# A tuned attention and mixture-of-experts kernel: the weights' maxima over the partitions go from TensorE and VectorE to a GpSimd library call

## The chip, the cores and the metric

The kernel runs on one core of one Trainium2 chip. A core has TensorE (PE in the profile, with its weight loads as PEld), VectorE (DVE), ScalarE (ACT), GpSimd (POOL) and SyncE (SP), which issues the DMAs. Each engine takes its instructions in the order of its own program and waits at semaphores for the others. The metric is the device time of one execution in microseconds, the median over runs.

## The reference

Three layers follow one another, all in float32:

```python
# 1. clustered attention: q, k, v (2, 8, 768, 64); a score counts only where the
#    nearest of 16 centroids of the query and of the key is the same one
# 2. h = x @ w_in; g = h * clip(h + 3, 0, 6) / 6; x = g @ w_out      (1536 tokens, 512 -> 2048 -> 512)
# 3. eight experts, all of them for every token:
    logits = x @ w_gate
    P = np.exp(logits - logits.max())
    for _ in range(8):
        P /= P.sum(1, keepdims=True) + 1e-09
        P /= P.sum(0, keepdims=True) + 1e-09
        P *= N / E
    for e in range(E):
        h = np.maximum(x @ w1[e], 0.0)      # 512 -> 1024
        out += P[:, e:e + 1] * (h @ w2[e])  # 1024 -> 512
```

## The kernel before

TensorE multiplies float16. A float32 matrix is therefore scaled by a power of two and split into a high and a low float16 part, and three products of parts stand for one float32 product. The power of two comes from the largest absolute value of the whole matrix. So before a weight can be split, one number has to be found over all 128 partitions and be known on each of them.

How that number is found: the pieces of a weight matrix are reduced along each partition by VectorE as they come (`amax`, L235 for a second weight w2 and L1308 for a first weight w1), eight values a partition in the tile `mx`. `top_steps` (L92) makes the rest in five steps: (a) VectorE reduces the eight to one in a column of the tile `pad` (L99); (b) TensorE transposes `pad` into spare columns of a PSUM bank (L75); (c) VectorE reduces the 128 columns to the maximum (L80); (e) TensorE multiplies that by the identity, which puts it on every partition (L85, two records each); and the last step hands it to `scale_of` (L121 to L130), which makes the scale `ws_s`. Beside the weights, `top_steps` serves other tensors (`x2`, the logits `lg`, the gate).

The third layer runs as 64 units, `unit(u)`, eight for each expert e: four quarters of the hidden features by two halves of the tokens. A unit has seven products (L1488 to L1491, six matmuls of 384 columns each) that build two PSUM accumulators X and Y, a Strassen-like scheme of seven products instead of eight. ScalarE copies an accumulator when a partial sum is needed later (`snap`, L1496), VectorE adds it (`u`, L1503), ScalarE and VectorE make the hidden parts `hh` and `hl` (L1507, L1508). The bank of a unit's Y becomes the X of the next unit. Behind each product stands a slot, `fill(0)` to `fill(6)`, with one or two groups of three matmuls of 512 columns of the unit before (L1437 to L1439, the second weight's product), and with whatever the plan puts there.

`plan_expert(e)` (L1401) writes the plan for expert e, while expert e-1 is computed: `at2(u, slot, f)` puts a step behind a slot's matmul groups, `at2_first` ahead of them, and `at_hops` puts the five steps of `top_steps` half a slot apart. With u = 8 (e - 1), the second weight w2 (names `w{n}_1`, printed `w_1_...` in the order below) has its last partial maximum in unit u+1, slot 4, and its five steps in slots 5 and 6 of that unit and slot 0 of the next; it is then split from unit u+2 on (L244 on ScalarE, L247 on VectorE). The first weight w1 (`w{n}_0`) has its last partial maximum in unit u+4, slot 6, and its steps in slots 0 to 2 of unit u+5. Its four quarters are then combined by GpSimd (`c0`, `c1`, tiles `cmb`, L1325 to L1331), scaled by ScalarE (`hi`, L1340, into `wop`) and completed by VectorE (`lo`, L1344): quarter 0 from slot 2 of unit u+5, its `hi` of the combined rows in slot 6.

GpSimd also makes four differences of the input for the second half of the tokens, for each token half (`diff`, L1066, tiles `xt`, by number T1 to T4); those of the second half lie in the first units of expert 0, beside the plan of expert 1. ScalarE (`hi`, L1079) and VectorE (`lo`, L1086) split them.

Of the kernel before, what the change touches and what calls it, by code (L numbers as in the profile page):

```python
# [8 lines left out]
F32 = mybir.dt.float32  # L9
# [4 lines left out]
ALU = mybir.AluOpType  # L14
AX = mybir.AxisListType
PSUM = bass.MemoryType.PSUM

P = 128
NJ = 6
# [11 lines left out]
def attention_moe_kernel(  # L31
# [16 lines left out]
    nc = tc.nc  # L48
# [43 lines left out]
    def top_steps(cols, col, name, room, then):  # L92


        d = {}

        def a():
            x = cols()
            nc.vector.tensor_reduce(pad[:, col:col + 1], x, axis=AX.X if len(x.shape) == 2 else AX.XY, op=ALU.max)  # L99

        def b():
            d["rows"], start = room(P)
            red_rows(d["rows"], start)

        def c():
            d["r"] = red_max(d.pop("rows"), name)

        def e():
            d["m"], start = room(1)
            to_all(d.pop("r"), d["m"], start, col)  # L110

        return [a, b, c, e, lambda: then(d.pop("m"))]

    def scale_of(m, n, target, name, keep, cap=None, bufs=1):

# [82 lines left out]
    def weight_tasks(n, m, pool, raw=None):  # L198

        src = layers[n][m]  # L200
        wide = src.dtype != F32
        rows, cols = src.shape
        nr = rows // P
        NP = 8
        d = {}
        nm = f"w{n}_{m}"

        def view(t, i):

            return t.rearrange("p a f -> p (a f)")[:, 512 * i:512 * (i + 1)]  # L210

        def start():
            d["raw"] = raw
            if raw is None:
                d["raw"] = mp.tile([P, nr, cols], F32, tag="raw", name=f"{nm}_raw", bufs=1)
            d["mx"] = small.tile([P, NP], F32, tag="w_mx", name=f"{nm}_mx")
            if not wide:
                nc.sync.dma_start(d["raw"], src.rearrange("(c p) f -> p c f", p=P))

        def load(i):  # L220
            r, o = divmod(512 * i, cols)
            d["c", i] = wide_tile(
                wdec2, src[P * r:P * r + P, o:o + 512].bitcast(U32), f"{nm}_c{i}", [512], bufs=WB)

        def dec0(i):
            d["t", i] = decode0(wdec2, d["c", i], f"{nm}_t{i}", bufs=3)

        def dec1(i):
            decode1(d["t", i])

        def dec2(i):
            decode2(d.pop(("c", i)), d.pop(("t", i)), view(d["raw"], i))

        def amax(i):
            nc.vector.tensor_reduce(  # L235
                d["mx"][:, i:i + 1], view(d["raw"], i), axis=AX.X, op=ALU.max, apply_absolute_value=True)

        def scale1(m1):
            d["s"], wsc[n, m] = scale_of(m1, 1, 2 + m, f"ws{m}", small, bufs=4)
            wsp[n, m] = pool.tile(  # L240
                [P, 2, nr, cols], F16, tag="ws", name=f"{nm}_s", bufs=1 if pool is wpool else 2)

        def hi(i):
            nc.scalar.activation(view(wsp[n, m][:, 0], i), view(d["raw"], i), AF.Copy, scale=d["s"][:, 0:1])  # L244

        def lo(i):
            nc.vector.scalar_tensor_tensor(  # L247
                out=view(wsp[n, m][:, 1], i), in0=view(d["raw"], i), scalar=d["s"][:, 0:1],
                in1=view(wsp[n, m][:, 0], i), op0=ALU.mult, op1=ALU.subtract)

        def piece(i):
            if not wide:
                return idle, idle, idle, idle, lambda: amax(i), idle
            return (lambda: load(i), lambda: dec0(i), lambda: dec1(i), lambda: dec2(i), lambda: amax(i), idle)

        def lo_pool(i):

            v = view(d["raw"], i)
            nc.scalar.activation(v, v, AF.Copy, scale=d["s"][:, 0:1])
            nc.gpsimd.tensor_tensor(out=view(wsp[n, m][:, 1], i), in0=v, in1=view(wsp[n, m][:, 0], i), op=ALU.subtract)  # L260

        parts = []
        for i in range(NP):
            parts += [(0.05, lambda i=i: hi(i)), (0.2, lambda i=i: lo_pool(i)) if (n, m) == (1, 0) else (0.7, lambda i=i: lo(i))]
        scale = top_steps(lambda: d["mx"], 1, nm, spare if n > 2 else room1, scale1)
        return start, [("m", piece(i)) for i in range(NP)], scale, parts

    def pipeline(pieces, depth):
# [655 lines left out]
    for g in range(-LEAD, NU + LAG + 16):  # L924
        i, u = divmod(g, NJ)
# [371 lines left out]
    def expert_w1(e):  # L1297

        n = 2 + e
        d = {}  # L1300

        def load():
            d["raw"] = mp.tile([P, KD, 1024], F32, tag="raw", name=f"w{n}_0_raw", bufs=1)
            d["mx"] = small.tile([P, 8], F32, tag="w_mx", name=f"w{n}_0_mx")
            nc.sync.dma_start(d["raw"], w1[e].rearrange("(c p) f -> p c f", p=P))

        def amax(i):
            nc.vector.tensor_reduce(  # L1308
                d["mx"][:, i:i + 1], d["raw"][:, i // 2, 512 * (i % 2):512 * (i % 2) + 512],
                axis=AX.X, op=ALU.max, apply_absolute_value=True)  # L1310

        def scale1(m1):
            d["s"], wsc[n, 0] = scale_of(m1, 1, 2, "ws0", small, bufs=4)

        def pair(i):
            x = {}

            def a(f, c):
                o = P * (i + 4 * f)
                return d["raw"][:, 2 * c:2 * c + 2, o:o + P]  # L1320

            def c0():
                s = x["s"] = epool.tile([P, 4, 2, P], F32, tag="cmb", name=f"cmb{e}_{i}", bufs=2)
                x["w"] = wop[e, i] = epool.tile([P, 2, 7, 2, P], F16, tag="wop", name=f"wop{e}_{i}", bufs=5)
                nc.gpsimd.tensor_tensor(out=s[:, 0], in0=a(1, 0), in1=a(1, 1), op=ALU.add)  # L1325
                nc.gpsimd.tensor_tensor(out=s[:, 2], in0=a(0, 0), in1=a(1, 0), op=ALU.subtract)

            def c1():
                s = x["s"]
                nc.gpsimd.tensor_tensor(out=s[:, 1], in0=s[:, 0], in1=a(0, 0), op=ALU.subtract)  # L1330
                nc.gpsimd.tensor_tensor(out=s[:, 3], in0=a(0, 1), in1=s[:, 1], op=ALU.subtract)  # L1331

            def parts():
                yield slice(A11, A12 + 1), d["raw"][:, :, P * i:P * i + P].rearrange("p (a c) f -> p a c f", a=2)
                yield A22, a(1, 1)
                yield slice(S1, S4 + 1), x["s"]

            def hi(k):
                o, v = list(parts())[k]
                nc.scalar.activation(x["w"][:, 0, o], v, AF.Copy, scale=d["s"][:, 0:1])  # L1340

            def lo(k):
                o, v = list(parts())[k]
                nc.vector.scalar_tensor_tensor(  # L1344
                    out=x["w"][:, 1, o], in0=v, scalar=d["s"][:, 0:1], in1=x["w"][:, 0, o],
                    op0=ALU.mult, op1=ALU.subtract)

            return [
                (0.1, c0), (0.1, c1), (0.1, lambda: hi(0)), (0.7, lambda: (lo(0), hi(1))),
                (0.4, lambda: (lo(1), hi(2))), (1.2, lambda: lo(2))]  # L1350

        return (
            load, [(0.65, lambda i=i: amax(i)) for i in range(8)],
            top_steps(lambda: d["mx"], 1, f"w{n}_0", spare if e else room1, scale1),
            [pair(i) for i in range(4)])


# [32 lines left out]
    def at2(u, slot, f):  # L1390
        plan2.setdefault((u, slot), []).append(f)
# [4 lines left out]
    def at_hops(u, slot, steps):  # L1396

        for n, f in enumerate(steps):
            v, k = divmod(slot + (n + 1) // 2, 7)
            (at2 if n % 2 == 0 else at2_first)(u + v, k, f)  # L1400

    def plan_expert(e):

        u = 8 * (e - 1)
        start, pcs, sc, parts = prep_matrix(2 + e, 1)
        at2(u - 1, 6, start)
        for k, (_, p) in enumerate(pcs):
            at2(u + (k + 4) // 7, (k + 4) % 7, p[4])
        at_hops(u + 1, 5, sc)
        for k in range(8):  # L1410
            at2(u + 2 + k // 7, k % 7, parts[2 * k][1])
            at2(u + 2 + (k + 1) // 7, (k + 1) % 7, parts[2 * k + 1][1])
        load, mx, sc, prs = expert_w1(e)
        at2(u + 3, 2, load)
        for k, f in enumerate(mx):
            at2(u + 4, max(0, k - 1), f[1])
        at_hops(u + 5, 0, sc)
        for i, (v, k) in enumerate(((5, 2), (6, 0), (6, 4), (7, 1))):
            for f in prs[i]:
                at2(u + v, k, f[1])  # L1420
                v, k = (v, k + 1) if k < 6 else (v + 1, 0)
# [131 lines left out]
    for u in range(NU2):  # L1553
        e = u // 8
# [53 lines left out]
```

## Time and profile before

| what | value |
|---|---|
| median of 3 runs | 1584.22 us (1580.78 to 1585.2) |
| profiled execution, its own time | 1583.48 us |
| its span, first to last instruction | 1581.7 us |
| TensorE busy | 1441.0 us, 91% of the span |
| VectorE busy | 975.2 us, 62% |
| ScalarE busy | 653.4 us, 41% |
| GpSimd busy | 345.6 us, 22% |
| DMA queue of the data | 86.15 MB, 19.9% of 16 engines' span |

Busy time adds up an engine's instructions. Matmuls are pipelined and their modelled records overlap: a matmul of 512 columns has a record of 0.38 us, and the next one starts 0.22 us later. What TensorE loses is therefore read from the distance between the starts of neighbouring matmuls and not from busy time. The expert stage lies from about 600 us to the end.

### The profile page before, as it was taken

To read this page: it belongs to the slowest core of one execution; us is meant where nothing else is said; L and a number is where in the kernel's file an instruction comes from. 1 tells how busy PE (TensorE), PEld (TensorE's weight loads), DVE (VectorE), ACT (ScalarE), POOL (GpSimd) and SP (SyncE) were. 2 spreads that over 40 slices of the span, in tenths; PEclk is the share of its full clock that TensorE was granted. 3 is DMA by queue.
4 is the path that set the end of the run, shared out by engine and by line. 5 is a ranking of instruction groups with operands and counts; after the bars stand their busy time and mean duration, and the time that the engine had idled before them with its cause. 6 is when DMAs were issued, how large, how long until landed. Compare 5 with 4: busy or idle time off the path is not lost.

```text
span 1581.7 us, 22923 instructions
## 1 busy us (share of the span) xinstructions
PE 1441.0 (91%) x9331; PEld 771.8 (49%) x9331; DVE 975.2 (62%) x1769; ACT 653.4 (41%) x1088; POOL 345.6 (22%) x313
## 2 busy tenths in 40 slices
PE   3778877897999798989999999999999999999999
PEld 1456555543444344445555555555555555555554
DVE  7888878886765667565456455455555554655332
ACT  2667756455443344334334323323323323324221
POOL 1568867443110321100010020020011011011000
PEclk9989978798999999999999999999999999999999
DMA  9387453231311010101101101101001011010011
GB/s 221 78 153 168 84 106 68 56 130 43 130 46 59 30 54 1 54 1 53 54 1 54 54 0 54 46 9 54 25 30 53 5 50 53 1 54 1 1 40 41
DMA packets 106633, 87.60 MB, mean 55 GB/s; under 512 B 78368, under 2 KB 88608, under 8 KB 106528
## 3 DMA queue, kind: packets, MB, share of 16 engines
q1 hardware_dynamic: 106528, 86.15, 19.9%
q8 instruction: 73, 1.20, 0.3%
q14 instruction: 32, 0.26, 0.1%
HBM read 64.01 MB, written 3.15 MB: 42 GB/s over the span
## 4 chain that ended last, share of the span: by engine, by line
PE 70%; DVE 20%; ACT 4%; issue 3%; DMA 1%; SPq 0%; DVEq 0%; ACTq 0%
PE o L1437 10%; PE o L1439 10%; PE o L1438 10%; PE X L1488 5%; PE X L1491 5%; PE X L1490 5%; PE Y L1491 4%; PE Y L1488 4%; PE Y L1490 4%; DVE pmt L650 3%; PE l L1220 3%; PE pmt L647 2%; PE l L888 2%; PE l L889 2%; PE l L890 1%
## 5 line engine op out<-in xcount | busy, mean ns | idle before, releaser
L1439 PE MATMUL o<-w_s,hl 128*128 128x512 f16 x768 | 291.9, 380 | 0.0
L1438 PE MATMUL o<-w_s,hh 128*128 128x512 f16 x768 | 291.8, 380 | 0.0
L1437 PE MATMUL o<-w_s,hh 128*128 128x512 f16 x768 | 291.7, 380 | 0.0
L1507 ACT ACTIVATE hh<-u 128x384 f16<-128x384 f32 x192 | 100.3, 523 | 373.3 <-DVE u L1503 373.3
L1325 POOL TENSOR_TENSOR cmb<-w_raw 128x256 f32<-128x256 f32 x32 | 24.1, 753 | 822.9 <-DMA w_raw<-in_moe_w_dram 379.5
L718 POOL TENSOR_TENSOR El<-E,Eh 128x768 f16<-128x768 f32 x92 | 160.8, 1758 | 115.5 <-ACT Eh L716 50.3
L1508 DVE SCALAR_TENSOR_TENSOR hl<-u,hh 128x384 f16<-128x384 f32 x192 | 112.3, 585 | 113.1 <-ACT hh L1507 113.1
L1503 DVE TENSOR_TENSOR u<-X,snap 128x384 f32<-128x384 f32 x64 | 35.7, 557 | 194.7 <-PE X L1491 194.7
L1490 PEld LDWEIGHTS <-wop 128*128 128x128 f16 x896 | 87.8, 98 | 88.1 <-issue 8.2
L1488 PEld LDWEIGHTS <-wop 128*128 128x128 f16 x896 | 87.8, 98 | 81.8 <-issue 0.7
L1503 DVE TENSOR_TENSOR u<-Y,snap 128x384 f32<-128x384 f32 x128 | 70.7, 552 | 82.0 <-PE Y L1491 82.0
L1439 PEld LDWEIGHTS <-hl 128*128 128x128 f16 x768 | 75.2, 98 | 91.1 <-issue 0.8
L1220 PE MATMUL l<-hh,w_s 128*128 128x512 f16 x384 | 118.6, 380 | 0.0
L704 ACT ACTIVATE E<-pS,esc 128x768 f32<-128x768 f32 x96 | 86.2, 898 | 77.1 <-PE pS L700 73.9
L1491 PEld LDWEIGHTS <-wop 128*128 128x128 f16 x896 | 87.7, 98 | 58.2 <-issue 0.3
L1496 ACT COPY snap<-X 128x384 f32<-128x384 f32 x128 | 61.2, 478 | 124.2 <-PE X L1491 122.8
L1437 PEld LDWEIGHTS <-hh 128*128 128x128 f16 x768 | 78.0, 102 | 64.8 <-issue 0.3
L1438 PEld LDWEIGHTS <-hh 128*128 128x128 f16 x768 | 75.2, 98 | 65.1 <-issue 0.4
L650 DVE TENSOR_REDUCE pmt<-pmt 128x1 f32<-128x768 f32 x84 | 80.7, 961 | 30.2 <-PE pmt L647 29.2
L647 PE MATMUL pmt<-kA,qA 80*128 80x384 f16 x184 | 53.4, 377 | 48.5 <-DVE pmt L650 20.4
L1220 PEld LDWEIGHTS <-w_s 128*128 128x128 f16 x576 | 56.6, 99 | 68.1 <-issue 1.1
L1488 PE MATMUL X<-xop,wop 128*128 128x384 f16 x256 | 83.4, 326 | 2.3 <-DVE u L1503 0.9
(280 smaller groups left out, 2997.5 us busy)
## 6 DMA issues: line engine op xcount, KB each, us to landing
w_raw<-in_moe_w_dram SPq DMA_DIRECT2D x16, 2048.0 KB, 8.8
w_c<-in_moe_w_out_dram SPq DMA_DIRECT2D x16, 512.0 KB, 3.6
w00x<-in_moe_w_in_dram SPq DMA_DIRECT2D x8, 512.0 KB, 5.6
w00f<-in_moe_w_in_dram SPq DMA_DIRECT2D x8, 512.0 KB, 3.8
w_c<-in_moe_w_in_dram SPq DMA_DIRECT2D x8, 512.0 KB, 3.9
qraw<-in_q_dram SPq DMA_DIRECT2D x8, 384.0 KB, 3.6
kraw<-in_k_dram SPq DMA_DIRECT2D x8, 384.0 KB, 4.2
vraw<-in_v_dram SPq DMA_DIRECT2D x2, 1536.0 KB, 9.9
```

What stands on the lines that cost most here:

```text
L650: nc.vector.tensor_reduce(nmx[i][:, j:j + 1], ps[:, :, 0:N2], axis=AX.XY, op=ALU.max, negate=True)
L718: eng.tensor_tensor(out=El, in0=E, in1=Eh, op=ALU.subtract)
L1220: nc.tensor.matmul(po[i], lhsT=a, rhs=r, start=(f == 0 and z == 0), stop=(f == NFC - 1 and z == 2))
L1437: nc.tensor.matmul(pe2[t], lhsT=a, rhs=wh, start=first, stop=False)
L1438: nc.tensor.matmul(pe2[t], lhsT=a, rhs=wl, start=False, stop=False)
L1439: nc.tensor.matmul(pe2[t], lhsT=b, rhs=wh, start=False, stop=last)
L1488: nc.tensor.matmul(o[:, 0:XT], lhsT=wh, rhs=xh, start=(first and c == 0), stop=False, skip_group_check=True)
L1490: nc.tensor.matmul(o[:, 0:XT], lhsT=wh, rhs=xl, start=False, stop=False, skip_group_check=True)
L1491: nc.tensor.matmul(o[:, 0:XT], lhsT=wl, rhs=xh, start=False, stop=(c == 1), skip_group_check=True)
L1503: nc.vector.tensor_tensor(h, src, r[k], op=ALU.add)
L1507: nc.scalar.activation(hh, src, AF.Relu)
L1508: nc.vector.scalar_tensor_tensor(out=hl, in0=src, scalar=0.0, in1=hh, op0=ALU.max, op1=ALU.subtract)
```

## The change

For the two weights of experts 1 to 7, fourteen maxima, the five steps become two. In the first, `partition_all_reduce` on GpSimd takes the tile `mx` (128 partitions by 8) and writes to every partition, column by column, the maximum over the partitions. In the second, one slot later, VectorE reduces these eight to one and calls `scale_of`. The weights of expert 0, of the second layer and all other users keep `top_steps`.

```diff
@@ -110,6 +111,21 @@
             to_all(d.pop("r"), d["m"], start, col)
 
         return [a, b, c, e, lambda: then(d.pop("m"))]
+
+    def top_library(cols, name, then):
+
+        d = {}
+
+        def a():
+            d["m8"] = small.tile([P, 8], F32, tag="w_m8", name=f"{name}_m8")
+            nc.gpsimd.partition_all_reduce(d["m8"], cols(), channels=P, reduce_op=RED.max)
+
+        def b():
+            m1 = small.tile([P, 1], F32, tag="w_m1", name=f"{name}_m1")
+            nc.vector.tensor_reduce(m1, d.pop("m8"), axis=AX.X, op=ALU.max)
+            then(m1)
+
+        return [a, b]
...
-        scale = top_steps(lambda: d["mx"], 1, nm, spare if n > 2 else room1, scale1)
+        scale = top_library(lambda: d["mx"], nm, scale1) if n > 2 else top_steps(
+            lambda: d["mx"], 1, nm, room1, scale1)
         return start, [("m", piece(i)) for i in range(NP)], scale, parts
...
-            top_steps(lambda: d["mx"], 1, f"w{n}_0", spare if e else room1, scale1),
+            top_library(lambda: d["mx"], f"w{n}_0", scale1) if e else top_steps(
+                lambda: d["mx"], 1, f"w{n}_0", room1, scale1),
             [pair(i) for i in range(4)])
...
-        at_hops(u + 1, 5, sc)
+        at2(u + 1, 5, sc[0])
+        at2(u + 1, 6, sc[1])
...
-        at_hops(u + 5, 0, sc)
+        at2(u + 5, 0, sc[0])
+        at2(u + 5, 1, sc[1])
```

The call belongs to another GpSimd library than `tensor_tensor`, so the program that is built holds loads of libraries, which the code does not show. They stand as `ISA` without names ahead of the instruction that needs them. In GpSimd's order around expert 1's two maxima stood before the last two of the differences (`xt`) and the combinations of the first quarter:

```order
L1066 TENSOR_TENSOR xt_1_7151<-acc,xt_1_7094 128x768
L1066 TENSOR_TENSOR xt_1_7193<-acc 128x768
L1325 TENSOR_TENSOR cmb_0_7772<-w_0_raw 128x256
L1326 TENSOR_TENSOR cmb_0_7772<-w_0_raw 128x256
L1330 TENSOR_TENSOR cmb_0_7772<-cmb_0_7772,w_0_raw 128x256
```

and now, in the changed kernel's line numbers:

```order
L1083 TENSOR_TENSOR xt_1_7151<-acc,xt_1_7094 128x768
L121 ISA
L121 ISA w_1_m_7173<-w_1_mx 128x8
L1083 ISA
L1083 TENSOR_TENSOR xt_1_7200<-acc 128x768
L121 ISA
L121 ISA w_0_m_7699<-w_0_mx 128x8
L1342 ISA
L1342 TENSOR_TENSOR cmb_0_7770<-w_0_raw 128x256
L1343 TENSOR_TENSOR cmb_0_7770<-w_0_raw 128x256
L1347 TENSOR_TENSOR cmb_0_7770<-cmb_0_7770,w_0_raw 128x256
```

Expert 1 has four loads. The last difference (T3) now stands behind a call and two loads, and the combinations of quarter 0 behind the second call and a load. For experts 2 to 7 there are two loads each, one ahead of w2's call, behind the fourth quarter's combinations of the expert before, and one ahead of the combinations of quarter 0: sixteen loads in all.

On TensorE, at the end of a unit in which w2's maximum is made (expert 2's), stood the transpose between a product and the group behind it, and the broadcast behind the next product:

```order
L1491 MATMUL X_8241<-xop_6633,wop_1_7883 128x384
L75 MATMUL Y_8260<-ident,pad 128x128
L1437 LDWEIGHTS hh_2_8228
L1437 MATMUL o_0_2_8326<-w_1_s,hh_2_8228 128x512
...
L1491 MATMUL X_8366<-xop_6633,wop_2_7956 128x384
L85 MATMUL X_8366<-ident,w_1_r 128x1
L1437 LDWEIGHTS hh_3_8322
```

and now there:

```order
L1511 MATMUL X_8371<-xop_6633,wop_2_7954 128x384
L1457 LDWEIGHTS hh_2_8355
L1457 MATMUL o_0_2_8324<-w_1_s,hh_2_8355 128x512
L1458 LDWEIGHTS hh_2_8355
L1458 MATMUL o_0_2_8324<-w_1_s,hh_2_8355 128x512
```

Nothing but the 28 instructions of the steps (b) and (e) left TensorE's program. On VectorE stood at the same place:

```order
L1508 SCALAR_TENSOR_TENSOR hl_1_8340<-u_1_8337,hh_1_8339 128x384
L99 TENSOR_REDUCE pad<-w_1_mx 128x1
L1508 SCALAR_TENSOR_TENSOR hl_2_8357<-X_8241,hh_2_8356 128x384
L80 TENSOR_REDUCE w_1_r<-Y_8260 128x1
L121 TENSOR_SCALAR ws_e<-X_8366 128x1
L122 TENSOR_SCALAR ws_e<-ws_e 128x1
```

and now:

```order
L1528 SCALAR_TENSOR_TENSOR hl_1_8338<-u_1_8335,hh_1_8337 128x384
L1528 SCALAR_TENSOR_TENSOR hl_2_8356<-X_8239,hh_2_8355 128x384
L125 TENSOR_REDUCE w_1_m_8362<-w_1_m_8347 128x1
L137 TENSOR_SCALAR ws_e<-w_1_m_8362 128x1
L138 TENSOR_SCALAR ws_e<-ws_e 128x1
```

The reduction that waits for the call stands where the reduction of the transposed column stood, and the four steps of the scale follow it at once.

## Rows read from the trace of the kernel before

**Rows 1.** Page: chain of work that ended last, shares of the span by engine.
```profile
PE 70%; DVE 20%; ACT 4%; issue 3%; DMA 1%; SPq 0%; DVEq 0%; ACTq 0%
```

**Rows 2.** Stretch: length; PE, PEld, DVE, ACT, POOL busy; clock, DMA share, GB/s.
```profile
820.00:940.00 120.00, 117.70 (x628) 61.05 (x627) 64.76 (x117) 44.44 (x82) 11.68 (x16) 1.00 0.10 36
```

**Rows 3.** One line's instructions: duration ns min/median/max, first and last start (us).
```profile
L75 PE MATMUL Y<-ident,pad x15: 327/330/332, 622.1 to 1411.3; 128*128 128x128 f32 x15
```

**Rows 4.** Timeline of TensorE, w2's steps: start us, us, instruction [idle <- releaser].
```profile
878.01 0.33 PE L1491 MATMUL X<-xop,wop 128*128 128x384 f16 x1
878.59 0.33 PE L75 MATMUL Y<-ident,pad 128*128 128x128 f32 x1 [0.26 <-DVE pad L99]
...
881.40 0.38 PE L85 MATMUL X<-ident,w_r 128*128 128x1 f32 x2 [0.57 <-ACT snap L1496]
881.65 0.38 PE L1437 MATMUL o<-w_s,hh 128*128 128x512 f16 x1
```

**Rows 5.** Timeline of TensorE, the same place two units on, without such steps.
```profile
894.46 0.33 PE L1491 MATMUL X<-xop,wop 128*128 128x384 f16 x1
...
896.24 0.38 PE L1437 MATMUL o<-w_s,hh 128*128 128x512 f16 x1
```

**Rows 6.** Timeline of TensorE, w1's steps.
```profile
927.54 0.33 PE L1491 MATMUL Y<-xT,wop 128*128 128x384 f16 x1
928.58 0.33 PE L75 MATMUL Y<-ident,pad 128*128 128x128 f32 x1 [0.72 <-DVE u L1503]
...
931.81 0.38 PE L85 MATMUL X<-ident,w_r 128*128 128x1 f32 x2 [0.62 <-ACT snap L1496]
932.05 0.38 PE L1437 MATMUL o<-w_s,hh 128*128 128x512 f16 x1
```

**Rows 7.** Timeline of TensorE, the same slots one unit on, without such steps.
```profile
944.21 0.33 PE L1491 MATMUL Y<-xT,wop 128*128 128x384 f16 x1
...
945.67 0.33 PE L1488 MATMUL X<-xT,wop 128*128 128x384 f16 x1
...
946.64 0.38 PE L1437 MATMUL o<-w_s,hh 128*128 128x512 f16 x1
```

**Rows 8.** Timeline of VectorE: w2's last partial maximum and its scale; w1's last partial maximum.
```profile
876.17 0.68 DVE L235 TENSOR_REDUCE w_mx<-w_raw 128x1 f32<-128x512 f32 x1
881.82 0.16 DVE L121 TENSOR_SCALAR ws_e<-X 128x1 int32<-128x1 int32 x1 [2.18 <-PE X L85]
...
926.39 0.68 DVE L1308 TENSOR_REDUCE w_mx<-w_raw 128x1 f32<-128x512 f32 x1
```

**Rows 9.** Timeline of ScalarE: quarter 0's combined rows, and the copy behind them.
```profile
941.07 1.14 ACT L1340 ACTIVATE wop<-cmb,ws_s 128x1024 f16<-128x1024 f32 x1
942.30 0.48 ACT L1496 COPY snap<-X 128x384 f32<-128x384 f32 x1
```

**Rows 10.** One tile's instructions (cmb): duration ns min/median/max, first and last start.
```profile
L1330 POOL TENSOR_TENSOR cmb<-cmb,w_raw x32: 717/726/1435, 519.5 to 1441.1; 128x256 f32<-128x256 f32 x32
```

**Rows 11.** Line L786's instructions, GpSimd's library load (POOLq is its sequencer).
```profile
L786 POOLq MODIFY_POOL_CONFIG  x2: 11/11/11, 0.7 to 0.8; - x2
L786 POOL IOTA dsc<- x1: 141/141/141, 0.8 to 0.8; 128x16 int32 x1
```

**Rows 12.** DMA issues: count, KB each, median us to landing.
```profile
w_raw<-in_moe_w_dram SPq DMA_DIRECT2D x16, 2048.0 KB, 8.8
w00x<-in_moe_w_in_dram SPq DMA_DIRECT2D x8, 512.0 KB, 5.6
```

**Rows 13.** Timeline of GpSimd: a small memset, then the difference T4 of expert 1's stretch.
```profile
1.24 0.10 POOL L789 MEMSET one<- 128x1 f32 x1
...
616.57 1.81 POOL L1066 TENSOR_TENSOR xt<-acc,xt 128x768 f32<-128x768 f32 x1 [20.60 <-DVE xT L1086]
```

**Rows 14.** Timeline of TensorE: the product behind slot 3 in that unit.
```profile
633.75 0.33 PE L1488 MATMUL X<-xop,wop 128*128 128x384 f16 x1
```

**Rows 15.** ScalarE's busy us (count) from T3's high part to the second copy.
```profile
627.02:630.92 3.90, 2.54 (x6) 1.00 0.00 0
```

More of the change, by code (lines that the diff above doesn't have):

```diff
@@ L16 @@
 PSUM = bass.MemoryType.PSUM
+RED = bass.bass_isa.ReduceOp
 P = 128
```

## The prediction

> **What bounds the kernel now.** I read the chain of waits first: most of what ends last is TensorE [rows 1]. Then the busy times of a stretch in the expert stage: TensorE is busy for 117.7 of 120 us at a granted clock of 1.00, which is the upper of its two levels, 2.4 GHz; VectorE for 64.8, ScalarE 44.4, GpSimd 11.7 [rows 2]. So in this stage time is what TensorE spends or loses, and the others have room if nobody waits for one late result. Then I looked at what the steps to be removed do to TensorE. The transposes into a bank Y start between 622.1 and 1411.3 us; they are fifteen, one of which belongs to the logits and stays [rows 3]. Seven are w2's and seven w1's. Busy time understates such a place, because records overlap. I therefore compare the same stretch of the program with and without the steps, from start to start.
>
> Around w2's steps, from the last matmul of a unit's seventh product to the first matmul behind the next unit's first product, TensorE takes 881.65 - 878.01 = 3.64 us [rows 4]; two units on the same run of instructions takes 896.24 - 894.46 = 1.78 us [rows 5]. The difference of 1.86 us is the price of w2's steps. In it lie a wait until VectorE has written `pad`, the transpose, and a wait until ScalarE's copy has left the accumulator whose spare columns the broadcast writes [rows 4]. Around w1's steps it is 932.05 - 927.54 = 4.51 us [rows 6] against 946.64 - 944.21 = 2.43 us [rows 7], a price of 2.08 us; there the transpose waits for VectorE's `u`, and the broadcast for the copy [rows 6].
>
> **What goes.** For w1, seven times 2.08 = 14.6 us; for w2, six times 1.86 = 11.2 us; expert 1's w2 is costed by itself below, because two of its loads meet other work. Together 25.8 us, all of it TensorE's own time. VectorE exchanges a reduction over 128 columns for one over eight, and loses a small one; it has room and I cost that at nothing.
>
> **What comes: the call.** The trace has no partition reduction and no GpSimd instruction of this kind. Below, a memset of one column takes 0.10 us; above, a subtraction of 128 by 768 takes 1.81 us [rows 13]. Eight columns with an exchange between partitions lie between; I take the middle, 1.0 us. The Trainium skill, page GPSIMD Engine Reference, section 3.2 (Cross-partition), gives 247,699 ns for a reduction along partitions at [128, 2048]; eight columns of that would be an estimated 0.97 us, and the sum would stay. What waits for the call is VectorE, in order, and behind its reduction stand the scale and the next unit's `u` and `hl`, for which ScalarE and then TensorE wait. w2's last partial maximum ends at 876.17 + 0.68 = 876.85; its scale began at 881.82, after VectorE had stood idle for 2.18 us [rows 8]. Moved forward by the 1.86 us won, the same point is 879.96, so a call of up to 3.1 us makes VectorE no later than it is. One of 1.0 us costs nothing.
>
> **What comes: the loads.** Sixteen library loads stand in GpSimd's order. Their cost is the term that decides. The only load in the trace is a pair of configuration instructions of 11 ns each at 0.7 to 0.8 us, and the instruction that needs it starts at 0.8 us [rows 11]: below, a load is free. But this was the first load of the program, and it may have found its code in place. Above, a load fetches code through a DMA; the transfers in the trace land after 5.6 us (512 KB) to 8.8 us (2 MB) [rows 12]. A library is code and not a weight matrix, so I take the smaller of these, 5.6 us, and keep 0 and 8.8 for the range. The Trainium skill, GPSIMD Engine Reference, section 2.1 (Instruction dispatch), gives about 5.95 us for the load of a kernel's code ahead of its first call; with that the sum below would be 0.7 us longer.
>
> Where do the loads lie? For experts 2 to 7 the one ahead of w2's call stands behind the fourth quarter's combinations, planned for slot 2 of unit u-1, while the call stands in slot 5 of unit u+1: 17 slots of about 120 / 56 = 2.1 us [rows 2], with nothing else on GpSimd. It is hidden at every price here. The one behind w1's call is not hidden so easily: it starts when the call ends, and quarter 0's combinations, which the old order made early, stand behind it. w1's last partial maximum ends at 926.39 + 0.68 = 927.07 [rows 8]. Call and load take C + L, the four additions 4 x 0.73 = 2.9 us [rows 10]; then ScalarE needs 1.14 us for the combined rows and 0.48 for the copy that stands behind them [rows 9]. TensorE needs that copy when it adds into X in slot 2, which began at 945.67 [rows 7] and now would begin 2.08 us earlier, at 943.59. With 0.1 us between the two on ScalarE this leaves C + L = 943.59 - 927.07 - 2.9 - 1.7 = 11.9 us. With 1.0 + 5.6 it is met by 5 us, and I cost these seven loads at nothing. Beyond 11.9 each microsecond costs seven.
>
> Against this stands a rule of the Trainium skill (GPSIMD Engine Reference, section 8, Key points): GpSimd shares its interfaces to SBUF with VectorE, and the two contend. The additions show it: median 726 ns, longest 1435 [rows 10]. The rule and this row agree. Moved from an early, quiet place into a busy one, all four may take twice as long, which brings the limit down to about 9.1 us; the sum stays, the upper end of the range grows.
>
> Expert 1 has the two loads that meet other work. The difference T4 ends at 616.57 + 1.81 = 618.38 [rows 13]. Behind it now stand a load, the call, another load, and T3 with 1.81 us: T3 is ready at 620.2 + 2L + C. ScalarE, in order, splits T3 and then has work until the second copy of that unit's X, 2.54 us in all [rows 15], and TensorE can add into X behind that, which it did at 633.75 [rows 14]. The delay is 620.2 + 2L + C + 2.54 - 633.75 = 2L + C - 11.0. With 5.6 and 1.0 it is +1.2 us; the gain of this place's own steps is swallowed. It is not below -1.9, the price of w2's steps elsewhere, and with L = 8.8 and C = 1.8 it is +8.4.
>
> **Sum.** 1.2 - 14.6 - 11.2 = -24.6 us. The profiled execution took 1583.48 us, 0.74 below the median of the runs; 1558.9, or 1559.6 against that median. With free loads -27.7, so 1556.5. With L = 8.8 and C = 1.8 it is -17.4, so 1566.8; with doubled additions as well, 7 x 1.5 = 10.5 us more, so 1577.3.
>
> **Rivals.** First, the load is paid inside the first call and not during the wait ahead of it. Then w2's call of experts 2 to 7 answers only at 876.85 + 6.6 = 883.45, 3.5 us after 879.96. If TensorE felt all of that, it would be 6 x 3.5 = 21 us and the time 1580.6: no change. For it speaks that the wait for the maximum stands on the call itself; against it, that no gap of the kind follows the load in the trace [rows 11], and that VectorE, half idle [rows 2], can make good a lateness before TensorE needs it. The section 2.1 named above speaks of such a first call that pays; this trace does not show one.
>
> Second, slower than before: the return load behind w1's call is long. The place is quarter 0 of each of seven experts; the chain is load, additions, ScalarE's combined rows, ScalarE's copy, TensorE. It makes the kernel slower where 25.8 = (2L + 1 - 11.0) + 7 (L + 1 - 11.9), at L = 12.5 us. If unloading and loading were each a transfer of 8.8 us [rows 12], L = 17.6, the terms would be 25.2 + 46.9 - 25.8 = +46.3 us and the time 1630.5. Against it: one long transfer is already more than code should need. For it: nothing in the trace measures a load that finds other code in place.
>
> Third, the gain is real but some of it comes back in the first units, where TensorE waits for VectorE anyway, or through slower additions: 1567 to 1579.
>
> **How the numbers follow.** I give the forecast, 1556 to 1567 with 1559.6 as its time, 0.65; still less, since hidden waits go too, 0.04; the third rival 0.11; the first 0.08; the second 0.12. This measurement tells about 0.3% from no change, 4.8 us, so 1579.5 to 1589.0 is the same. Faster: 0.65 + 0.04 + 0.11 and a little of the first rival, 0.81; same 0.07; slower 0.12. The range from 1554 to 1577 leaves out the second rival, most of the first and the tails.
>
> **What would show it.** In the new profile the transposes into Y are down to the logits' one, and the stretches of rows 4 and 6 take about 1.8 and 2.4 us. The distance between neighbouring experts falls by about 3.9 us. The configuration pairs stand sixteen times more on GpSimd; behind w1's call the first addition of quarter 0 starts some 6.6 us after the last partial maximum, and ScalarE's combined rows wait little or not. TensorE's idle time appears once, near the place that was at 633.75, waiting for ScalarE. I am wrong if VectorE idles for GpSimd's call at each w2 and TensorE behind it, or if ScalarE's line for the combined rows shows a wait for GpSimd in every expert and TensorE waits for the copy behind it.

## The result and the profile after

| kernel | median of the runs | lowest to highest | ratio to before, with its 95% interval |
|---|---|---|---|
| before | 1584.3 us | 1580.78 to 1585.2 | |
| after | 1570.36 us | 1564.24 to 1571.12 | 0.9908 [0.9879, 0.9937] |

The kernel became 13.9 us faster, 0.9%, where 24.6 us were forecast; the time lies inside the range of 1554 to 1577. The profiled execution after took 1571.12 us with a span of 1569.3 us, 12.4 us less than the one before.

The page after, part 4, the shares of the chain that ended last, answers to [rows 1]:

```profile
PE 73%; DVE 17%; issue 3%; ACT 3%; DMA 0%; POOL 0%; DVEq 0%; ACTq 0%; POOLq 0%
```

TensorE has a larger share of a shorter chain, and GpSimd is as good as absent from it. The new and the changed instructions of GpSimd, as groups by line of the kernel after (duration in ns as least, median and most, then first and last start):

```profile
L121 POOL PARTITION_ALL_REDUCE w_m<-w_mx x14: 367/396/399, 628.5 to 1399.6; - x14
L121 POOLq MODIFY_POOL_CONFIG  x16: 1/11/15, 622.8 to 1313.7; - x16
...
L1083 POOLq MODIFY_POOL_CONFIG  x2: 108/108/108, 628.8 to 628.9; - x2
...
L1342 POOLq MODIFY_POOL_CONFIG  x14: 88/88/108, 689.8 to 1400.0; - x14
...
L1347 POOL TENSOR_TENSOR cmb<-cmb,w_raw x32: 718/904/1437, 524.1 to 1428.7; 128x256 f32<-128x256 f32 x32
```

The call takes 0.4 us, less than half of what was put down for it. The 16 loads show as 16 pairs of configuration instructions, 8 pairs ahead of calls and 8 ahead of `tensor_tensor`, as [rows 11] had one. The row of the pair hardly shows the load's cost: 108 ns at most. That stands in the idle time behind it. GpSimd at w1's maximum of expert 4 (timeline: start, duration, and idle time ahead of it with what ended it):

```profile
1049.36 0.37 POOL L121 PARTITION_ALL_REDUCE w_m<-w_mx  x1 [47.93 <-DVE w_mx L1325]
1056.87 0.72 POOL L1342 TENSOR_TENSOR cmb<-w_raw 128x256 f32<-128x256 f32 x1 [7.14 <-issue]
...
1058.24 1.04 POOL L1347 TENSOR_TENSOR cmb<-cmb,w_raw 128x256 f32<-128x256 f32 x1
...
1063.16 1.59 POOL L1348 TENSOR_TENSOR cmb<-w_raw,cmb 128x256 f32<-128x256 f32 x1
```

The idle time of 7.14 us is ended by "issue", that is by nothing the profile shows. It stands behind the configuration pair at this place in every expert, and I read it as the load. With the call, 1056.87 - 1049.36 = 7.5 us pass from the maximum to the first addition. TensorE feels none of it. The stage from expert 1 to the start of expert 7 in one row of each kernel (window; PE, PEld, DVE, ACT, POOL busy; clock, DMA share, GB/s), first before:

```profile
728.96:1453.07 724.11, 710.32 (x3781) 368.71 (x3780) 386.98 (x698) 254.96 (x475) 70.37 (x96) 1.00 0.10 36
```

and after:

```profile
740.15:1440.71 700.56, 700.56 (x3746) 366.35 (x3744) 387.80 (x686) 254.83 (x475) 88.04 (x108) 1.00 0.10 37
```

TensorE is now busy for the whole of 700.56 us. Both windows hold six experts, from the first product of expert 1 to that of expert 7: 120.69 us each before, 116.76 after. The stretches that took 3.64 and 4.51 us with steps [rows 4, 6] are down to what they are elsewhere [rows 5, 7]. TensorE after, the last matmul of a unit's seventh product to the group behind the next product (w2's place of expert 3), then the same of w1's place:

```profile
885.29 0.33 PE L1511 MATMUL X<-xop,wop 128*128 128x384 f16 x1
...
887.07 0.38 PE L1457 MATMUL o<-w_s,hh 128*128 128x512 f16 x1
...
932.97 0.33 PE L1511 MATMUL Y<-xT,wop 128*128 128x384 f16 x1
...
935.40 0.38 PE L1457 MATMUL o<-w_s,hh 128*128 128x512 f16 x1
```

They take 1.78 and 2.43 us, to the hundredth the values of [rows 5] and [rows 7]. Of the fifteen transposes into Y [rows 3] one is left, the logits'.

**Where the rest went.** The profiled executions can be added up by the first products of the experts:

| stretch | before | after | difference |
|---|---|---|---|
| ahead of expert 0 | 592.46 | 596.25 | +3.8 |
| expert 0 | 136.50 | 143.90 | +7.4 |
| experts 1 to 6 | 724.11 | 700.56 | -23.6 |
| expert 7 and the end | 128.6 | 128.6 | 0.0 |

The sum is -12.4 us, that of the profiled executions. Nothing that the change touches lies ahead of expert 0; over the twelve profiles that point lies anywhere from 591.1 to 596.5 us, with the library and without. Of the +7.4 of expert 0 most is the change's own, and its first part is the place of T3. GpSimd in expert 0 after:

```profile
621.05 1.81 POOL L1083 TENSOR_TENSOR xt<-acc,xt 128x768 f32<-128x768 f32 x1 [21.28 <-DVE xT L1103]
628.49 0.40 POOL L121 PARTITION_ALL_REDUCE w_m<-w_mx  x1 [5.63 <-ACT snap L1516]
635.68 1.79 POOL L1083 TENSOR_TENSOR xt<-acc 128x768 f32<-128x768 f32 x1 [6.79 <-issue]
```

ScalarE, in order, waits for T3 and has two more instructions ahead of the copy that TensorE needs:

```profile
637.50 0.94 ACT L1096 ACTIVATE xT<-xt,x_s 128x768 f16<-128x768 f32 x1 [7.11 <-POOL xt L1083]
638.34 0.51 ACT L1527 ACTIVATE hh<-u 128x384 f16<-128x384 f32 x1
638.76 0.71 ACT L260 ACTIVATE w_s<-w_raw,ws_s 128x512 f16<-128x512 f32 x1
639.37 0.46 ACT L1516 COPY snap<-X 128x384 f32<-128x384 f32 x1
```

and TensorE loses 4.75 us there, behind which its matmuls start at twice the distance:

```profile
634.75 0.38 PE L1459 MATMUL o<-w_s,hl 128*128 128x512 f16 x1
639.87 0.48 PE L1508 MATMUL X<-xop,wop 128*128 128x384 f16 x1 [4.75 <-ACT snap L1516]
...
641.11 0.53 PE L1510 MATMUL X<-xop,wop 128*128 128x384 f16 x1
641.43 0.53 PE L1511 MATMUL X<-xop,wop 128*128 128x384 f16 x1
```

The windows around that point show why (clock in the third column from the right):

```profile
637.70:644.50 6.80, 4.63 (x14) 2.08 (x14) 5.03 (x8) 4.87 (x9) 0.00 (x0) 0.50 0.00 0
644.50:651.30 6.80, 6.80 (x38) 3.53 (x36) 3.93 (x8) 3.34 (x6) 0.00 (x0) 1.00 0.01 2
```

The granted clock stood at its lower level, 1.2 GHz, for 6.8 us, the first 2.2 of them while TensorE still waited. Before, there was no such fall here. Measured from the first product of expert 0, the product behind the copy starts 639.87 - 596.25 = 43.6 us in, where before it was 633.75 - 592.46 = 41.3 [rows 14]: +2.3 us. By the start of unit 3, at 51.4 us against 46.8, the loss has grown to 4.6, half of it the clock's.

The other two parts lie in the softmax of the logits, units 4 and 5 of expert 0: +0.9 and +1.9 us, together with the 4.6 the 7.4. TensorE has only the small column sums there (L91) and waits for VectorE's chain. The +0.9 of unit 4 is the clock: its waits are the same before and after, but the clock is at the lower level for 3.4 us there before:

```profile
673.91:677.32 3.41, 3.17 (x9) 1.47 (x10) 2.62 (x10) 0.52 (x1) 0.00 (x0) 0.50 0.00 0
```

and for 6.8 us after:

```profile
682.05:688.88 6.83, 6.34 (x19) 3.08 (x20) 4.22 (x14) 1.49 (x3) 0.00 (x0) 0.50 0.00 1
```

That is not shown to be the change's: two of the kernels below that make expert 1's w1 by the five steps have the 6.8 us too, and one with the call has 3.4. The +1.9 of unit 5, where w1's maximum of expert 1 is made, is the call's: in the twelve profiles unit 5 takes 19.6 us wherever the five steps make that maximum, and 21.1 us or more wherever the call does. VectorE after:

```profile
696.06 0.15 DVE L125 TENSOR_REDUCE w_m<-w_m 128x1 f32<-128x8 f32 x1
...
696.75 0.15 DVE L1175 TENSOR_SCALAR b_ct<-Y 128x8 f32<-128x8 f32 x1
696.94 0.20 DVE L1176 RECIPROCAL b_ct<-b_ct 128x8 f32<-128x8 f32 x1
697.18 0.54 DVE L1177 TENSOR_SCALAR b_ct<-b_ct 128x8 f32<-128x8 f32 x1
697.75 0.74 DVE L1178 TENSOR_TENSOR pr<-pr,b_ct 128x96 f32<-128x96 f32 x1
...
704.77 0.17 DVE L1177 TENSOR_SCALAR b_ct<-b_ct 128x8 f32<-128x8 f32 x1
704.98 0.26 DVE L1178 TENSOR_TENSOR pr<-pr,b_ct 128x96 f32<-128x96 f32 x1
```

The maximum and the scale take 0.7 us of the chain, but the scale's four operations stand in it with the five steps as well, one column sum later. What is new is the length of small instructions: the same two take 0.54 and 0.74 us at 697 but 0.17 and 0.26 at 705. GpSimd made the eight additions of expert 1's quarters 0 and 1 from 696.97 to 702.85, behind its load; before, they had been done at 653 to 659.

### The profile page after: what moved, and what is told of

It is laid out like the page before. It is cut to its first block, busy times and chain, and to the rows that moved or that the text cites. A ratio compares the mean times of both kernels' runs of the same rounds, so it can differ in the third digit from the quotient of the medians.

```text
span 1569.3 us, 22865 instructions
## 1 busy us (share of the span) xinstructions
PE 1436.4 (92%) x9289; PEld 771.7 (49%) x9289; DVE 978.7 (62%) x1755; ACT 653.4 (42%) x1088; POOL 364.1 (23%) x327
## 2 busy tenths in 40 slices
DMA packets 106633, 87.60 MB, mean 56 GB/s; under 512 B 78368, under 2 KB 88608, under 8 KB 106528
## 4 chain that ended last, share of the span: by engine, by line
PE 73%; DVE 17%; issue 3%; ACT 3%; DMA 0%; POOL 0%; DVEq 0%; ACTq 0%; POOLq 0%
PE o L1458 10%; PE o L1459 10%; PE o L1457 10%; PE X L1508 5%; PE X L1511 5%; PE X L1510 5%; PE Y L1508 4%; PE Y L1510 4%; PE Y L1511 4%; PE l L1237 3%; DVE pmt L667 3%; PE l L906 2%; PE l L907 2%; PE l L905 2%; PE pmt L664 2%
## 5 line engine op out<-in xcount | busy, mean ns | idle before, releaser
L121 POOL PARTITION_ALL_REDUCE w_m<-w_mx x14 | 5.4, 385 | 572.4 <-DVE w_mx L1325 287.9
## 6 DMA issues: line engine op xcount, KB each, us to landing
vraw<-in_v_dram SPq DMA_DIRECT2D x2, 1536.0 KB, 10.2
```

## The experiments

Two theories stood against each other on where the missing gain went. A: it is given back in expert 1's two maxima (T3 behind two loads, and the softmax). B: the loads and the slower additions cost something everywhere, or the stage starts later because of the library.

**Expert 1 without the library.** Experts 2 to 7 call; expert 1 keeps the five steps for both weights.

```diff
-        scale = top_library(lambda: d["mx"], nm, scale1) if n > 2 else top_steps(
+        scale = top_library(lambda: d["mx"], nm, scale1) if n > 3 else top_steps(
...
-            top_library(lambda: d["mx"], f"w{n}_0", scale1) if e else top_steps(
+            top_library(lambda: d["mx"], f"w{n}_0", scale1) if e > 1 else top_steps(
...
```

> The library call serves experts 2 to 7 alone; expert 1's two maxima are made by the five steps as in the kernel before. Theory A: the changed kernel missed its forecast at one place, expert 1, where a difference of the input stands behind two library loads and ScalarE and TensorE wait, and where the granted clock falls after that wait; the twelve later maxima give 6 x (1.86 + 2.08) = 23.6 us. Then this kernel takes 1584.3 - 23.6 = 1560.7 us (1558 to 1564) and its trace has TensorE's granted clock at its upper level between the first product of the experts and the softmax of the logits as before. Rival B: the library costs something ahead of the expert stage, which began 3.8 us later in the changed kernel's profile; then it begins late here too and the time is about 1565.

Measured: 1562.13 us, ratio 0.9859 [0.9846, 0.9873]. Expert 0 takes 137.39 us, 6.5 less than after, and the six experts behind it 116.76 each as after. The first product of expert 0 starts at 592.7 us, as early as before, so B's later start is not the library's. Two library maxima fewer, and the kernel is faster: A.

**The call for w1 alone.** Expert 1's w1 calls, its w2 keeps the five steps; this parts the softmax from T3.

```diff
-        scale = top_library(lambda: d["mx"], nm, scale1) if n > 2 else top_steps(
+        scale = top_library(lambda: d["mx"], nm, scale1) if n > 3 else top_steps(
...
```

> The library call serves experts 2 to 7 and expert 1's first weight; expert 1's second weight keeps the five steps, so no load meets T3. It separates the softmax of the logits, beside which that first weight's maximum is made, from the place at T3. Theory A with nothing lost there: 1584.3 - 23.6 - 2.0 = 1558.7, 2 us below the kernel with the five steps for all of expert 1. Rival D, that what TensorE wins there it waits for the softmax's own chain: equal to that kernel within 1 us; and if the changed order costs the softmax something, 2 to 3 us above it.

Measured: 1564.26 us, 0.9871 [0.9858, 0.9884]; expert 0 takes 140.80 us. That is 3.4 us more than with the five steps for both, and 3.1 less than after; the medians are 2.1 us above the five steps, with intervals that overlap. So w1's call gives nothing in the softmax and costs something, the last branch of rival D. Not all of the 3.4 is the call's: in this run the clock was at its lower level for 3.4 us inside unit 5. There unit 5 takes 23.1 us, against 21.5 after and 19.6 with the five steps, both without such a fall inside it. TensorE at the third of unit 5's four column sums (L91); first with the call:

```profile
691.70 0.59 PE L91 MATMUL Y<-b_cs,one 128*128 128x8 f32 x2 [2.84 <-DVE b_cs L1166]
```

and with the five steps for both, where the broadcast stands just ahead of it:

```profile
690.18 0.38 PE L86 MATMUL X<-ident,w_r 128*128 128x1 f32 x2 [0.61 <-ACT snap L1522]
690.43 0.37 PE L91 MATMUL X<-b_cs,one 128*128 128x8 f32 x2
```

The wait here grows from 0.61 us, for the copy, to 2.84 for VectorE's sums, though two steps have left TensorE.

**T3 on VectorE.** All fourteen call; one subtraction leaves GpSimd, so T3 no longer stands behind the two loads.

```diff
-                nc.gpsimd.tensor_tensor(out=t, in0=x, in1=y, op=ALU.subtract)
+                (nc.vector if (bk, o) == (1, T3) else nc.gpsimd).tensor_tensor(out=t, in0=x, in1=y, op=ALU.subtract)
```

> As the changed kernel, but the difference T3 of the second token half is made by VectorE, so it does not stand behind a call and two loads on GpSimd; GpSimd then has two loads for expert 1 as for the others. Theory A: the wait of 4.9 us of TensorE for ScalarE near 635 us is gone, the fall of the clock behind it too, VectorE pays about 0.9 us more: 1559 to 1563 us. Rival C, VectorE's wait for the call itself is what delays expert 1's first units: the time stays within 2 us of the changed kernel's 1570.

Measured: 1560.54 us, 0.9848 [0.9834, 0.9861], faster than the kernel after. Expert 0 takes 136.72 us. ScalarE's wait for T3 at that place:

```profile
627.20 0.94 ACT L1096 ACTIVATE xT<-xt,x_s 128x768 f16<-128x768 f32 x1 [0.20 <-DVE xt L1083]
```

It is 0.20 us against 7.11. With T3 gone nothing stands between expert 1's two calls, so the load behind the first and the one ahead of the second are gone as well. The load that is left, ahead of w2's call, makes VectorE wait 1.2 us; TensorE's units 1 and 2 are still 2.2 us shorter than before.

**Both.** T3 on VectorE, and expert 1's w1 by the five steps.

```diff
+                (nc.vector if (bk, o) == (1, T3) else nc.gpsimd).tensor_tensor(out=t, in0=x, in1=y, op=ALU.subtract)
...
+            top_library(lambda: d["mx"], f"w{n}_0", scale1) if e > 1 else top_steps(
...
```

> T3 on VectorE as in the kernel that took 1560.5 us, and expert 1's first weight by the five steps: GpSimd then loads behind expert 1's first call and combines quarters 0 and 1 early, before the softmax of the logits. Theory G: beside the softmax the call cost time twice over, as the five operations of the maximum and scale stand in the softmax's chain on VectorE, and as the eight additions of GpSimd, moved behind the load, run beside that chain and lengthen its small operations (0.17 to 0.70 us, 0.26 to 0.74). Then 1560.5 - 2 = 1558.5 us (1557 to 1560). Rival H, the difference between the kernels with and without expert 1's first call was the granted clock's chance: equal to 1560.5 within 1 us.

Measured: 1559.54 us, 0.9841 [0.9825, 0.9857]. Expert 0 takes 135.08 us, the least of these kernels. In medians it can't be told from the kernel with T3 alone, so they do not part G from H. The traces do: no fall of the clock lies in unit 5 of either, and it takes 19.6 us here against 21.1 with T3 alone.

**The additions ahead of the call.** T3 on VectorE, all fourteen call, and the eight additions of expert 1's quarters 0 and 1 stand ahead of w1's call instead of behind its load.

```diff
+        if e == 1:
+            for f in prs[0][:2] + prs[1][:2]:
+                at2(u + 5, 0, f[1])
+            prs[0][:2] = prs[1][:2] = [(0.1, nothing)] * 2
```

> T3 on VectorE, expert 1 with both calls, and its quarters 0 and 1 combined ahead of the second call instead of behind it, so the additions lie before the softmax's chain as in the kernel before; the maximum and scale stay in the chain. It splits theory G in two. If GpSimd's additions beside the chain are what costs, 1.5 to 2 us go: 1558.5 to 1559. If the scale's operations are what costs, nothing goes: 1560.5. VectorE's b_ct operations show which: at 0.17 us each or up to 0.70.

Measured: 1559.91 us, 0.9836 [0.9821, 0.985]; expert 0 takes 136.39 us. The long ones among VectorE's small instructions are gone, while the maximum and the scale are still in the chain:

```profile
690.34 0.15 DVE L125 TENSOR_REDUCE w_m<-w_m 128x1 f32<-128x8 f32 x1
...
691.45 0.17 DVE L1177 TENSOR_SCALAR b_ct<-b_ct 128x8 f32<-128x8 f32 x1
691.66 0.26 DVE L1178 TENSOR_TENSOR pr<-pr,b_ct 128x96 f32<-128x96 f32 x1
```

So it was GpSimd's additions that lengthened them. TensorE's wait at the third column sum is the shorter for it, against 2.69 us after and 2.14 with T3 alone:

```profile
693.38 0.39 PE L91 MATMUL Y<-b_cs,one 128*128 128x8 f32 x2 [1.38 <-DVE b_cs L1166]
```

Expert 0's span is only 0.3 us below that with T3 alone, because 3.4 us at the lower clock level, all of them busy, lie in unit 5 of this run; the matmuls lose half of that, an estimated 1.7 us. Unit 5 takes 21.65 us, without this loss about 19.9: of the 1.5 us between 21.1 and 19.6 the additions are then 1.2. The medians don't tell it.

**The limit of 11.9 us.** The prediction had the loads of w1 free up to 11.9 us from the last maximum to the first addition. With T3 on VectorE, 27 or 60 memsets behind each w1 call of experts 2 to 7 put that number to the test.

```diff
             nc.gpsimd.partition_all_reduce(d["m8"], cols(), channels=P, reduce_op=RED.max)
+            if late:
+                for _ in range(27):
+                    nc.gpsimd.memset(pad, 0.0)
...
```

> T3 on VectorE, and for experts 2 to 7 27 memsets of an unused tile on GpSimd between w1's call and the load behind it, some 4 us, as if the load were 4 us longer. In the changed kernel call and load take about 7.6 us from the last partial maximum to the first addition; with 4 us more 11.6, under the limit of 11.9 that the prediction worked out. Theory: no change against 1560.5 (within 1.5 us; up to 8 us more if the additions meet VectorE and take twice as long). Rival: any delay of these additions reaches TensorE, 6 x 4 = 24 us more.

> The same with 60 memsets, some 9 us: 16.6 us from the last partial maximum to the first addition, 4.7 beyond the limit. Theory: 6 x 4.7 = 28 us more than 1560.5, so 1589 (1583 to 1600), slower than the kernel before, and TensorE waits at the product behind slot 1 of each unit u+6 for ScalarE's copy. Rival: the slack is larger than worked out (ScalarE or TensorE make it good): under 1570.

Measured: 1581.78 us, 0.9969 [0.9958, 0.998], and 1639.83 us, 1.0343 [1.0328, 1.0358]. The memset was taken for cheaper than it is: 0.26 us from one to the next. So the delays were 7.1 and 15.8 us. GpSimd and TensorE with 27:

```profile
1044.46 0.37 POOL L121 PARTITION_ALL_REDUCE w_m<-w_mx  x1 [47.93 <-DVE w_mx L1328]
1044.70 7.11 POOL L124 MEMSET pad<- 128x128 f32 x27
1058.81 0.72 POOL L1345 TENSOR_TENSOR cmb<-w_raw 128x256 f32<-128x256 f32 x1 [7.00 <-issue]
...
1060.67 0.38 PE L1462 MATMUL o<-w_s,hl 128*128 128x512 f16 x1
1063.29 0.32 PE L1511 MATMUL X<-xT,wop 128*128 128x384 f16 x1 [2.25 <-ACT snap L1519]
```

and with 60:

```profile
1064.97 0.37 POOL L121 PARTITION_ALL_REDUCE w_m<-w_mx  x1 [47.94 <-DVE w_mx L1328]
...
1081.17 0.38 PE L1462 MATMUL o<-w_s,hl 128*128 128x512 f16 x1
...
1088.21 0.71 POOL L1345 TENSOR_TENSOR cmb<-w_raw 128x256 f32<-128x256 f32 x1 [7.23 <-issue]
...
1092.69 0.48 PE L1511 MATMUL X<-xT,wop 128*128 128x384 f16 x1 [11.14 <-ACT snap L1519]
```

Maximum to addition takes 1058.81 - 1044.46 = 14.35 and 23.24 us, by 2.45 and 11.34 over the limit. TensorE, whose matmul of 512 columns lets the next one start 0.22 us later, loses 1063.29 - 1060.67 - 0.22 = 2.40 and 11.30 us. The limit holds to about a tenth of a us; both runs missed what was expected of them, the larger part by the memset's price. The 21 us of the first would nearly fit its rival's 24 too, but of a delay of 7.1 us TensorE feels only 2.4. What comes on top is the clock: with 60, an expert takes 129.6 us in the mean, 12.9 more than 116.76; 11.3 are the wait and 1.6 the matmuls at the lower level behind it. With 27, six waits make 14.8 us, and in three of the experts the clock fell as well.

**Is it the waits or TensorE's own instructions?** Three kernels without the library ask whether the 3.93 us an expert could have been had from the order alone. In the first, each of the five steps stands a slot behind the one before (expert 1's w1 as it was).

```diff
-        at_hops(u + 1, 5, sc)
+        for f, v, k in zip(sc, (1, 1, 1, 2, 2), (4, 5, 6, 0, 0)):
+            at2(u + v, k, f)
...
+            for f, v, k in zip(sc, (4, 5, 5, 5, 5), (6, 0, 1, 2, 3)):
+                at2(u + v, k, f)
```

> No library: the kernel before with its five steps farther apart, a whole slot each, for both weights of experts 1 to 7 (expert 1's first weight as before), so that TensorE finds the column written and the accumulator copied when it comes to a step. Theory E: of the 1.86 and 2.08 us that a maximum cost, most was TensorE's waits (0.42 and 0.73 at w2, 0.88 and 0.79 at w1) and not its instructions; then 7 x 1.15 + 6 x 1.67 = 18 us go and the time is 1566 (1562 to 1570). Rival F, TensorE waits at these steps wherever they stand, as its own instructions and the turnaround are what costs: 1580 to 1585.

Measured: 1583.92 us, 0.9998 [0.9989, 1.0007], no change; the 1566 of theory E are missed, and rival F's time holds. TensorE, w1's place:

```profile
929.37 0.30 PE L75 MATMUL X<-ident,pad 128*128 128x128 f32 x1 [0.52 <-DVE pad L99]
...
933.37 0.32 PE L1493 MATMUL X<-xT,wop 128*128 128x384 f16 x1 [1.43 <-DVE w_r L80]
```

The wait for the copy has gone and another has come: the next product needs the bank that holds the transposed column until VectorE has reduced it. In the second kernel only the broadcast moves, behind its slot's groups, for thirteen of the fourteen.

```diff
-            (at2 if n % 2 == 0 else at2_first)(u + v, k, f)
+            (at2 if n % 2 == 0 or n in behind else at2_first)(u + v, k, f)
...
-        at_hops(u + 1, 5, sc)
+        at_hops(u + 1, 5, sc, (3,))
```

> No library: the kernel before, with the broadcast of thirteen of the fourteen maxima (step e) behind the slot's matmul groups instead of ahead of them; expert 1's first weight as before. The prediction read TensorE's wait ahead of the broadcast, 0.73 to 0.79 us, as a wait for ScalarE's copy of the accumulator. If that is so, the copy is done when TensorE comes to the broadcast behind the groups, and 13 x 0.75 = 9.8 us go: 1575 (1573 to 1577). Rival: the wait belongs to the turnaround through VectorE and moves along to the next product: 1583 to 1585.

Measured: 1573.42 us, 0.9923 [0.991, 0.9936], close to the 1575 expected. An expert takes 118.96 us: with the wait for the copy 1.73 of the 3.93 us went. The whole change has 0.9908 [0.9879, 0.9937]: as it stands, with what it gives back in expert 0, it is not told from this one move. The third kernel also moves the first step a slot earlier.

```diff
-        at_hops(u + 1, 5, sc)
+        at2(u + 1, 4, sc[0])
+        at_hops(u + 1, 5, [idle] + sc[1:], (3,))
...
```

> No library: the kernel with the broadcast behind the groups (1573.4 us), and the first step, VectorE's column of pad, one slot earlier, right behind the last partial maximum. The transpose then finds its column written. If TensorE's wait ahead of the transpose, 0.42 us at w2 and 0.88 at w1 in the kernel before, is a wait for that column and for what VectorE does before it, 7 x 0.42 + 6 x 0.88 = 8.2 us go: 1565 (1563 to 1568), and what is left of a maximum is 0.3 us of wait for the reduction of the transposed column and some 0.3 of instructions. Rival: the wait stays, since VectorE is late with other work that TensorE needs there: 1572 to 1574.

Measured: 1573.26 us, 0.9921 [0.9907, 0.9935], nothing more gained; the 1565 expected are missed, and the rival held. TensorE, w2's place and then w1's:

```profile
876.76 0.27 PE L75 MATMUL Y<-ident,pad 128*128 128x128 f32 x1
878.29 0.32 PE L1490 MATMUL X<-xop,wop 128*128 128x384 f16 x1 [0.61 <-DVE w_r L80]
...
926.34 0.33 PE L75 MATMUL Y<-ident,pad 128*128 128x128 f32 x1 [0.72 <-DVE u L1505]
```

At w2's place the wait for `pad` is gone and the one for the reduction is there; at w1's the transpose waits for VectorE's `u`, which reads the bank that the transpose writes, and no earlier `pad` helps. So nearly half of the gain of an expert was in the order. None of these three orders got the rest; the change, which takes the steps off TensorE and out of its PSUM banks, did.

## Why the prediction was right, and where its size was off

**The steps on TensorE: right.** 1.86 + 2.08 = 3.94 us an expert was read from [rows 4 to 7]; 3.93 were measured, six times.

**The call: right that it is hidden, its size too high.** It takes 0.4 us, not 1.0. VectorE waited for it once, 1.1 us in expert 1. The first rival, a load paid inside the call, did not come.

**The loads: hidden as worked out, their size too low.** L is 5.6 us ahead of w2's call of expert 1 and 6.8 to 7.4 on the return, against 5.6 for both. The Trainium skill (GPSIMD Engine Reference, section 2.1, Instruction dispatch) has 5.95 us for the load that the first call of freshly loaded code pays; the return loads here are 0.8 to 1.5 us longer. The limit of 11.9 us was right, and the 4.4 us between it and the 7.5 measured are the reason why the second rival did not come.

**"Expert 1 ... With 5.6 and 1.0 it is +1.2 us": the place was right, the term too small.** It is +2.3 us: 2L + C was 5.63 + 0.40 + 6.79 = 12.8 where 12.2 stood, and T4 itself ended 0.7 us later in the stage (622.86 - 596.25 against 618.38 - 592.46). And it left out what a wait of 4.75 us does to the clock, another 2.2 us.

**"For w1, seven times 2.08": the term that was wrong in kind.** The seventh, expert 1's, lies in the softmax. There TensorE waits for VectorE, so leaving TensorE out gives nothing, and the additions behind the load lengthen VectorE's chain. It cost 1.9 us where a gain of 2.08 stood: 4.0 us. The prediction took a price read at other experts for a stretch with another limit, though its third rival named the very thing, "some of it comes back in the first units, where TensorE waits for VectorE anyway, or through slower additions". The 1570.4 us lie in that rival's 1567 to 1579, which had a chance of 0.11, and not in the forecast's 1556 to 1567.

**The contention: taken for GpSimd's loss alone.** The Trainium skill (GPSIMD Engine Reference, section 8, Key points) says that GpSimd shares its interfaces to SBUF with VectorE and contends with those of its instructions that have two inputs in SBUF or run in a mode with two ports. The trace agrees that they contend: the median of the additions of one line went from 0.73 us [rows 10] to 0.90. The limit left room for that. What cost time was the other side, VectorE's small instructions in the softmax.

Together: 23.6 us for the six experts, less 7.4 in expert 0, less 3.8 for a stage that began later in the profiled execution, 12.4. The 12.2 that are missing from the forecast there are 3.4 at T3's place (4.6 where 1.2 stood), 4.0 at the seventh w1, 0.9 of clock in unit 4 and the 3.8; the last two are not shown to be the change's. Of B the later start falls, since the kernel with five steps a slot apart and no library started at 595.2 us; so do costs everywhere, since TensorE is busy without a gap from 740 us on.

## What to carry to other kernels

A load of a library is free where the engine would have stood idle, and what it costs is told by the first needed instruction behind it: count the slack from the last input to that instruction's consumer, and move what does not fit to another engine, as with T3. A price that was read at one place holds only where the same engine sets the end; a first or last repetition that overlaps another phase must be costed by itself. Before a step is taken off an engine, its waits are worth a look: moving one instruction half a slot gave nearly half of the gain of an expert here.

## What the runs showed of the hardware

- `partition_all_reduce` of 128 by 8, a maximum that reaches every partition, takes only 0.37 to 0.40 us.
- Changing between this call and `tensor_tensor` costs GpSimd 5.6 to 5.8 us ahead of the call where it could be seen, and 6.7 to 7.7 on the way back, over all runs. The profile shows it as idle time ended by "issue"; the DMA packets are 106633 before and after, so they do not show it.
- GpSimd's additions beside VectorE's small float32 instructions lengthened the latter from 0.17 to 0.54 us and from 0.26 to 0.74 us. Not all of them: reciprocals of 128x8 and reductions of 128x96 beside the same additions kept their 0.20 and 0.25 us.
- An idle time of TensorE of 4.75 us had the lower clock level from its middle on, for 6.8 us; one of 11.3 us had it for 10.2 us, which also began while TensorE was idle; after that the clock was at 2.4 GHz again. With 27 memsets, beside each of the waits of 2.6, 2.8 and 2.9 us lay 3.4 us at the lower level, beside the three of 2.1 to 2.2 us none. The waits of the kernel before, up to 0.72 us each in [rows 4, 6], left it at 1.00 [rows 2].
